# First batch's x loaded in whole rows into one tile for two steps, and step 1's first-stage groups moved out of the border into the head and units 0 to 2 of step 0

## The chip, the core and the metric

One Trainium2 chip, of which the program uses one core. The metric is the device time in microseconds of one execution; a kernel's time is the median of several runs. One execution is also recorded by the hardware profiler, and all rows below are from that one. All times inside the kernel count from the first instruction of its span.

## What is computed

Three stages in float32 follow one another: a convolution by FFT along the sequence (8 batches of 3072 positions, 256 channels), a soft mixture of experts on the 24576 rows that come out, and a gated feed-forward block. Cut to what matters:

```python
def _attn_ref(x, filt_r, filt_i):                 # x: (8, 3072, 256), filters: (1537, 256)
    X = np.fft.rfft(x, axis=1)
    Y = X * (filt_r + 1j * filt_i)[None, :, :]
    return np.fft.irfft(Y, n=x.shape[1], axis=1)

def _moe_ref(x, phi, w1, w2):                     # x: (24576, 256), phi: (256, 32)
    logits = x @ phi
    d = softmax(logits, axis=0)                   # over the rows; slot_input = d.T @ x
    slot_out = relu(slot_input @ w1[e]) @ w2[e]   # 8 experts with 4 slots each
    return softmax(logits, axis=1) @ slot_out

def _moe2_ref(x, w_gate, w_val, w_out):
    g = x @ w_gate
    return (g * sigmoid(g) * (x @ w_val)) @ w_out
```

## The kernel before

The program has two phases, with a short transition between them. Phase 1 (the first 380 us or so) does the Fourier part and the reduction to expert slots; phase 2 does the gated block, on PE from end to end. The change touches the first 65 us of phase 1.

**Steps and units.** Phase 1 runs over 16 *steps*; step s is batch s // 2 and half s % 2 of the 256 channels. Each step has a *first stage*: the sequence of 3072 positions is cut as 48 x 64, and a DFT over the 48 is done in four *chunks* of 32 channels each (s1_chunk). A chunk is four matmuls into a PSUM tile s (L235), a transpose by DVE into sg (L243), and a copy by ACT into the step's tile b (spread, L252). All four chunks of a step must be in b before its *second stage*, which runs in six *units* (s2_unit): four matmuls X<-fwd,b (L263), two products by DVE with the filter ft (P at L267, Q at L268), and two combinations by GpSimd into yt (L276, L280). Two units later the results are turned by PE (T, L290, tr_unit), and every second unit is multiplied with phi (L, L298, phi_pair); both are evacuated by ACT.

**Filters.** The filter tile ft is itself made on the chip: load_filters fetches six tiles fraw, and turn_filters transposes four blocks on PE (fT, L202), from where ACT (L209) and DVE (L214, L216) copy them into ft. The six groups of the first channel half are turned ahead of step 0, those of the second half one by one in the units of step 0.

**x.** load_x(step, k) issues on SP two of a step's four transfers (L182): for k = 0 or 1 and for r = 0 and 1, 48 partitions (0 to 47, or 64 to 111) with 16 pieces of 128 floats, since a step uses half of the channels of a row. Two pools xp[0] and xp[1], of 16 KB in each partition, hold the x of even and odd steps. Step 0 is loaded first of all, then come the filters and fwd, then step 1, and step s + 2 is issued in units 0 and 2 of step s.

**Order.** The order of the instructions on each engine is the order in which they are written (a manual schedule), each engine works its queue off in order, and what an engine waits for is set by the tiles. SP issues all of these transfers, and reuses eight semaphores in turn, so a transfer also waits for the landing of the one eight places before it. Ahead of the first chunk, ten *idle* matmuls of a constant keep PE busy while x is on its way. In units of a step s from 1 on, chunks of step s + 1 are spread over the units by the tables late and plan, one PSUM buffer for all of them, except for the odd chunks of the first three steps, which use the buffer of the tag c. Step 1's chunks have no place in a unit: they stand in a row in **border**, which comes behind the last unit of step 0, with the last filter group and two of the T groups and an L that are due there; step 1's first unit begins behind it.

**Later uses.** The pool cvp, behind the x pools, holds the raw weights of the gated block, which are converted from unit 14 on (conv); inv, the constants of the inverse transform, is fetched at unit 8.

Of the kernel before, what the change touches and what calls it, by code (L numbers as in the profile page):

```python
# [80 lines left out]
def spectral_softmoe_glu_kernel(  # L81
# [56 lines left out]
    def phase1():  # L138
        with ExitStack() as c1:
# [3 lines left out]
            xp = []  # L143
            cvs = ExitStack()
            yp = [c1.enter_context(tc.tile_pool(name=f"yp{k}", bufs=1)) for k in range(3)]
# [27 lines left out]
            def load_x(step, k):  # L173
                b, h = divmod(step, 2)
                if b >= NB:
                    return

                if k == 0:
                    xt[step] = xp[step % 2].tile([128, 2, 16, 128], F32, tag="x", name="x")
                xr = x[b].rearrange("(p h r n) d -> r h p n d", h=2, r=2, n=16)  # L180
                for r in range(2):
                    nc.sync.dma_start(  # L182
                        out=xt[step][64 * r:64 * r + 48, k], in_=xr[r, k, :, :, h * 128:(h + 1) * 128]
                    )

            def load_filters():
# [34 lines left out]
            def s1_chunk(step, c):  # L221
# [4 lines left out]

                if step < 3 and c % 2:
                    ps = ps_c.tile([128, 1024], F32, tag="c", name="s1").rearrange("p (n d) -> p n d", d=32)
                else:
                    ps = ps_s1.tile([128, 32, 32], F32, tag="s1", name="s1")  # L230
# [17 lines left out]
            def spread():  # L248

                while staged:  # L250
                    step, c, sg = staged.pop(0)
                    act.copy(  # L252
                        bt[step][:, :, c * 32:(c + 1) * 32].rearrange("p (j k) d -> p j k d", k=2),
                        sg[:, 0:NJ // 2].rearrange("p j d k -> p j k d"),
                    )
# [358 lines left out]
            def conv():  # L614
# [6 lines left out]
                def load(n):  # L621
                    if n >= len(chunks):
                        return
                    i, c = chunks[n]
                    raws[n] = cvp.tile([128, cw, 2], I32, tag="raw", name="raw", bufs=2)
                    nc.sync.dma_start(
                        out=raws[n].rearrange("p n k -> p (n k)"),
                        in_=flat((w_gate, w_val, w_out)[i])[:, c * cw:(c + 1) * cw].bitcast(I32),
                    )
# [4 lines left out]
                for n, (i, c) in enumerate(chunks):  # L634
# [3 lines left out]
                    pair = (lambda a: a.rearrange("p (h m) -> p h m", h=2)) if i == 2 else (lambda a: a)  # L638
                    mag = cvp.tile([128, cw], I32, tag="mag", name="mag", bufs=2)
                    low = cvp.tile([128, cw], I32, tag="low", name="low", bufs=2)  # L640
                    act.activation(pair(mag.bitcast(F32)), halves(hf), AF.Copy, scale=2.0 ** -112)
# [63 lines left out]
            act.copy(expo, expo)  # L705
            xp += [cr.enter_context(tc.tile_pool(name=f"xp{k}", bufs=1, side="right")) for k in (1, 0)][::-1]
            cvp = cvs.enter_context(tc.tile_pool(name="cvp", bufs=1, side="right"))
            load_x(0, 0)
            load_x(0, 1)
            load_filters()  # L710
# [3 lines left out]
            for k in range(2):  # L714
                nc.sync.dma_start(out=fwd[:, 12 * k:12 * k + 12], in_=c_fwd[:, 12 * k:12 * k + 12])
                if k == 0:
                    nc.sync.dma_start(out=phi_sb, in_=phi.rearrange("(t p) e -> p t e", p=128))
            load_x(1, 0)
            load_x(1, 1)
            idle = ps_x.tile([128, 512], F32, tag="X", name="idle")  # L720
            for _ in range(10):
                pe.matmul(out=idle[:, 0:384], lhsT=ident, rhs=csm)
            for c in range(4):
                s1_chunk(0, c)
                spread()
            for q in range(6):
                turn_filters(0, q)
# [4 lines left out]
            units = [(s, u) for s in range(2 * NB) for u in range(6)]  # L732
            late = [[[], [], [], [], [], []], [[], [], [0], [1], [2, 3], []]]
            plan = [[], [0], [1], [2], [3], []]
# [24 lines left out]

            def border():  # L760

                turn_filters(1, 5)
                s1_chunk(1, 0)
                s1_chunk(1, 1)
                spread()
                s1_chunk(1, 2)
                tr_unit(0, 3)
                s1_chunk(1, 3)
                spread()
                phi_pair(0, 1)  # L770
                tr_unit(0, 4)
                bt.pop(0)

            def aside():
                next(side, None)

            for i, (s, u) in enumerate(units):
                if u in (0, 2):
                    load_x(s + 2, u // 2)
# [4 lines left out]
                s2_unit(s, u)  # L784
                if i == 5:
                    border()
                    continue
                if s == 0:
                    turn_filters(1, u)
                spread()  # L790
                if i != 6:
                    tail_ops(i)
                if i >= CONV_AT and i % 2 == 0:
                    aside()
                pump(1)
                for c in (plan if s > 1 else late[s])[u]:
                    s1_chunk(s + 1, c)
                if u == 5:
                    bt.pop(s)
# [440 lines left out]
```

## Time and profile before

| | |
|---|---|
| median of 3 runs | 1443.76 us (1441.32 to 1445.64) |
| profiled execution, its own time | 1444.62 us |
| its span, first to last instruction | 1442.2 us |
| PE busy | 98% of the span |
| x of step 0 has landed | 15.50 us |
| first X matmul of step 0, step 1, step 2 | 25.07, 45.87, 60.65 us |

The page gives busy shares of the engines over the span and in 40 slices of 36 us each; the slice rows show at a glance where an engine is not busy, and how many GB/s the transfers moved. The chain of work that ended last tells, for a stretch, what each moment was waiting for. A view of stretches gives the busy time of each engine, the granted clock and the transfer rate between two points in time. A timeline lists instructions in order with the idle time before each and what ended it. PE is the matmul engine, PEld its weight loads, SPq the queue of SP that issues transfers.

### The profile page before, as it was taken

To read this page: it belongs to the slowest core of one execution; us is meant where nothing else is said; L and a number is where in the kernel's file an instruction comes from. 1 tells how busy PE (TensorE), PEld (TensorE's weight loads), DVE (VectorE), ACT (ScalarE), POOL (GpSimd) and SP (SyncE) were. 2 spreads that over 40 slices of the span, in tenths; PEclk is the share of its full clock that TensorE was granted. 3 is DMA by queue.
4 is the path that set the end of the run, shared out by engine and by line. 5 is a ranking of instruction groups with operands and counts; after the bars stand their busy time and mean duration, and the time that the engine had idled before them with its cause. 6 is when DMAs were issued, how large, how long until landed. Compare 5 with 4: busy or idle time off the path is not lost.

```text
span 1442.2 us, 22675 instructions
## 1 busy us (share of the span) xinstructions
PE 1410.8 (98%) x8441; PEld 1099.1 (76%) x8441; DVE 1139.3 (79%) x1760; ACT 911.1 (63%) x1673; POOL 258.7 (18%) x334
## 2 busy tenths in 40 slices
PE   7999999999999999999999999999999999999998
PEld 4566666656488888888888888888888888888887
DVE  4777888777388888878987897888789788877776
ACT  3567667764366667666666766676666667666664
POOL 1577677653210000000000000000000000000000
PEclk9999999999999999999999999999999999999999
DMA  9978988869811221221032023013111221221111
GB/s 227 184 138 156 158 146 136 169 152 375 281 28 30 44 55 30 44 55 30 16 73 41 15 37 78 15 30 65 35 30 30 59 41 29 45 45 26 19 30 30
DMA packets 178364, 116.25 MB, mean 81 GB/s; under 512 B 105264, under 2 KB 161456, under 8 KB 178128
## 3 DMA queue, kind: packets, MB, share of 16 engines
q1 hardware_dynamic: 176768, 112.92, 38.8%
q10 hardware_dynamic: 1104, 1.11, 0.3%
q8 instruction: 66, 1.08, 0.3%
q0 software_dynamic: 384, 0.79, 0.2%
q14 instruction: 42, 0.34, 0.1%
HBM read 68.13 MB, written 34.60 MB: 71 GB/s over the span
## 4 chain that ended last, share of the span: by engine, by line
PE 88%; DVE 5%; DMA 4%; ACT 2%; issue 1%; POOL 0%; SPq 0%; ACTq 0%; DVEq 0%; POOLq 0%
PE o L1115 53%; PE V L1078 9%; PE G L1077 9%; PE X L263 4%; PE s L235 3%; PE T L290 2%; DMA raw<-in_moe_w_out_dram 2%; DVE sg L243 1%; PE c L531 1%; PE L L298 1%; DMA x<-in_x_dram 1%; PE o L1135 1%; DMA fwd<-in_const_fwd_dram 1%; DVE P L267 1%; PE c L371 1%
## 5 line engine op out<-in xcount | busy, mean ns | idle before, releaser
L1115 PE MATMUL o<-hi,wo 128*128 128x512 f32 x2256 | 694.6, 389 | 0.0
L1080 ACT ACTIVATE s<-G 128x512 f32<-128x512 f32 x576 | 344.5, 598 | 328.2 <-PE G L1077 324.3
L1086 DVE TENSOR_TENSOR h<-V,s 128x512 f32<-128x512 f32 x576 | 393.7, 684 | 152.7 <-ACT s L1080 150.1
L1115 PEld LDWEIGHTS o<-hi,wo 128*128 128x128 f32 x2256 | 423.5, 188 | 87.6
L1115 PE MATMUL o<-lo,wo 128*128 128x512 f32 x1128 | 438.9, 389 | 0.3 <-DVE lo L1094 0.3
L1094 DVE TENSOR_TENSOR lo<-h,hi 128x512 fp32r<-128x512 f32 x576 | 419.8, 729 | 0.7
L1093 ACT CAST hi<-h 128x512 fp32r<-128x512 f32 x576 | 354.1, 615 | 36.8 <-DVE h L1086 35.2
L1115 PEld LDWEIGHTS o<-lo,wo 128*128 128x128 f32 x1128 | 211.8, 188 | 44.9 <-DVE lo L1094 0.7
L1078 PE MATMUL V<-c,v 128*128 128x512 f32 x576 | 224.6, 390 | 1.6 <-DVE h L1086 1.6
L1077 PE MATMUL G<-c,g 128*128 128x512 f32 x576 | 224.5, 390 | 0.3 <-ACT s L1080 0.3
L263 PEld LDWEIGHTS X<-fwd,b 128*128 128x128 f32 x768 | 92.9, 191 | 55.9 <-issue 38.4
L1078 PEld LDWEIGHTS V<-c,v 128*128 128x128 f32 x576 | 108.0, 188 | 25.5 <-DVE h L1086 3.5
L1077 PEld LDWEIGHTS G<-c,g 128*128 128x128 f32 x576 | 108.0, 188 | 24.2 <-ACT s L1080 1.2
L243 DVE STREAM_TRANSPOSE sg<-s 128x1024 f32<-128x1024 f32 x64 | 78.7, 1235 | 53.0 <-PE s L235 52.1
L1029 POOL TENSOR_TENSOR lg<-lg,mx 96x1024 f32<-96x1024 f32 x7 | 16.8, 2403 | 555.3 <-DVE mx L1027 555.3
L263 PE MATMUL X<-fwd,b 128*128 128x128 f32 x768 | 108.8, 285 | 3.6 <-ACT b L252 3.5
L252 ACT COPY b<-sg 128x768 f32<-128x768 f32 x64 | 59.1, 923 | 69.1 <-DVE sg L243 69.1
L276 POOL TENSOR_TENSOR yt<-P 128x256 f32<-128x256 f32 x96 | 70.4, 733 | 104.7 <-DVE P L267 103.6
L1120 DVE STREAM_TRANSPOSE ot<-o 128x512 f32<-128x512 f32 x94 | 65.0, 713 | 29.5 <-PE o L1115 29.5
L235 PE MATMUL s<-x,csm 48*64 48x512 f32 x512 | 72.6, 611 | 3.6 <-DVE sg L243 3.4
L267 DVE TENSOR_TENSOR P<-X,ft 128x512 f32<-128x512 f32 x96 | 64.7, 674 | 10.1 <-PE X L263 9.2
L280 POOL TENSOR_TENSOR yt<-Q 128x256 f32<-128x256 f32 x95 | 69.8, 734 | 0.4
(207 smaller groups left out, 991.5 us busy)
## 6 DMA issues: line engine op xcount, KB each, us to landing
x<-in_x_dram SPq DMA_DIRECT2D x64, 384.0 KB, 8.5
out_dram<-ot SPq DMA_DIRECT2D x188, 128.0 KB, 2.8
w<-in_moe_w_dram SPq DMA_DIRECT2D x16, 512.0 KB, 7.9
w<-in_moe_w_dram SPq DMA_DIRECT2D x8, 1024.0 KB, 11.1
c<-ch SPq DMA_DIRECT2D x42, 128.0 KB, 2.4
c<-cl SPq DMA_DIRECT2D x42, 128.0 KB, 2.4
raw<-in_moe_w_gate_dram SPq DMA_DIRECT2D x12, 256.0 KB, 5.5
raw<-in_moe_w_val_dram SPq DMA_DIRECT2D x12, 256.0 KB, 5.5
```

The source lines that it names most:

```text
L235: pe.matmul(out=ps[64 * k:64 * k + 64, 16 * r:16 * r + 16, :], lhsT=s1t_sb[64 * r:64 * r + 48, :], rhs=xt[step][64 * r:64 * r + 48, k, :, ...
L243: dve.transpose(out=sg.rearrange("p j d k -> p d j k"), in_=ps.rearrange("p n d -> p d n"))
L263: pe.matmul(out=ps[:, g].rearrange("p r m -> p (r m)"), lhsT=bb[:, j, :], rhs=fwd[:, j, :])
L267: dve.tensor_tensor(out=P, in0=ps, in1=f, op=ALU.mult)
L276: pool.tensor_tensor(out=y[:, :, 0, :], in0=P[:, :, 0, :], in1=P[:, :, 1, :], op=ALU.subtract)
L1077: pe.matmul(out=pg, lhsT=g4[c][:, fs], rhs=c4[b][:, q, G, :])
L1078: pe.matmul(out=pv, lhsT=v4[c][:, fs], rhs=c4[b][:, q, G, :])
L1080: act.activation(s, pg, AF.Silu)
L1086: dve.tensor_tensor(out=h, in0=pv, in1=s, op=ALU.mult)
L1093: act.copy(hi, h)
L1094: dve.tensor_tensor(out=lo, in0=h, in1=hi, op=ALU.subtract)
L1115: pe.matmul(out=a[h], lhsT=w[:, k, h], rhs=m, start=(f == 0 and n == 0), stop=(f == NF - 1 and n == 2), skip_group_check=True,)
```

## The change

The first batch's x is now fetched by load_pair into one tile x01 with room for both halves of the channels (32 KB in each partition, where later both x pools lie): four transfers, each of 48 partitions with one contiguous piece of 16 KB. Steps 0 and 1 read their halves of it. The x pools and cvp are opened (open_xp) behind unit 2 of step 0, when step 1's last chunk has been issued, and x of step 2 is issued there, all four transfers at once. The function border is gone: step 1's chunk 0 is done in the head, ahead of the filter transposes, chunks 1 to 3 in units 0 to 2 of step 0 through the table late, and the T and L groups go into the ordinary places (tail_ops). Six idle matmuls are issued instead of ten. The odd chunks of step 1 use the common PSUM buffer, since the other one serves the filter groups there.

```diff
             xp = []
-            cvs = ExitStack()
+            cvs, x01, cvps = ExitStack(), ExitStack(), []
...
+            def load_pair():
+
+                t = x01.enter_context(tc.tile_pool(name="x01", bufs=1, side="right")).tile(
+                    [128, 2, 16, D], F32, tag="x01", name="x01"
+                )
+                xr = x[0].rearrange("(p h r n) d -> r h p n d", h=2, r=2, n=16)
+                for k in range(2):
+                    for r in range(2):
+                        nc.sync.dma_start(out=t[64 * r:64 * r + 48, k], in_=xr[r, k])
+                for h in range(2):
+                    xt[h] = t[:, :, :, h * 128:(h + 1) * 128]
+
+            def open_xp():
+
+                x01.close()
+                xp.extend(
+                    [cr.enter_context(tc.tile_pool(name=f"xp{k}", bufs=1, side="right")) for k in (1, 0)][::-1]
+                )
+                cvps.append(cvs.enter_context(tc.tile_pool(name="cvp", bufs=1, side="right")))
...
-                if step < 3 and c % 2:
+                if step in (0, 2) and c % 2:
...
-            xp += [cr.enter_context(tc.tile_pool(name=f"xp{k}", bufs=1, side="right")) for k in (1, 0)][::-1]
-            cvp = cvs.enter_context(tc.tile_pool(name="cvp", bufs=1, side="right"))
-            load_x(0, 0)
-            load_x(0, 1)
+            load_pair()
             load_filters()
...
-            load_x(1, 0)
-            load_x(1, 1)
             idle = ps_x.tile([128, 512], F32, tag="X", name="idle")
-            for _ in range(10):
+            for _ in range(6):
                 pe.matmul(out=idle[:, 0:384], lhsT=ident, rhs=csm)
             for c in range(4):
                 s1_chunk(0, c)
                 spread()
+            s1_chunk(1, 0)
+            spread()
...
-            late = [[[], [], [], [], [], []], [[], [], [0], [1], [2, 3], []]]
+            late = [[[1], [2], [3], [], [], []], [[], [], [0], [1], [2, 3], []]]
...
-            def border():
-
-                turn_filters(1, 5)
-                s1_chunk(1, 0)
-                s1_chunk(1, 1)
-                spread()
-                s1_chunk(1, 2)
-                tr_unit(0, 3)
-                s1_chunk(1, 3)
-                spread()
-                phi_pair(0, 1)
-                tr_unit(0, 4)
-                bt.pop(0)
...
-                if u in (0, 2):
+                if s and u in (0, 2):
                     load_x(s + 2, u // 2)
                 if i == 8:
                     nc.sync.dma_start(out=inv, in_=c_inv)
                 if i >= CONV_AT and i % 2:
                     aside()
                 s2_unit(s, u)
-                if i == 5:
-                    border()
-                    continue
                 if s == 0:
                     turn_filters(1, u)
                 spread()
-                if i != 6:
-                    tail_ops(i)
+                tail_ops(i)
                 if i >= CONV_AT and i % 2 == 0:
                     aside()
                 pump(1)
                 for c in (plan if s > 1 else late[s])[u]:
                     s1_chunk(s + 1, c)
+                if i == 2:
+                    open_xp()
+                    load_x(2, 0)
+                    load_x(2, 1)
```

On SP, from the start of phase 1 (x and x_145 are loads of x, fraw and nyq filters, fwd, phi_sb and inv constants). Before:

```order
L182 DMA x<-in_x_dram 48x16x128 x4
L192 DMA fraw<-in_filt_r_dram 128x1024
...
L192 DMA fraw<-in_filt_i_dram 128x1024
L711 DMA nyq<-in_filt_r_dram 128x2x1
L715 DMA fwd<-in_const_fwd_dram 128x1536
L717 DMA phi_sb<-in_moe_phi_dram 128x2x32
L715 DMA fwd<-in_const_fwd_dram 128x1536
L182 DMA x<-in_x_dram 48x16x128 x12
L781 DMA inv<-in_const_inv_dram 128x3072
```

After, at the same place:

```order
L194 DMA x_145<-in_x_dram 48x4096 x4
L212 DMA fraw<-in_filt_r_dram 128x1024
...
L212 DMA fraw<-in_filt_i_dram 128x1024
L728 DMA nyq<-in_filt_r_dram 128x2x1
L732 DMA fwd<-in_const_fwd_dram 128x1536
L734 DMA phi_sb<-in_moe_phi_dram 128x2x32
L732 DMA fwd<-in_const_fwd_dram 128x1536
L182 DMA x<-in_x_dram 48x16x128 x8
L784 DMA inv<-in_const_inv_dram 128x3072
```

The four first transfers are twice as large, and the transfers of x behind fwd are eight instead of twelve; the first of these eight waits for PE.

On PE in the head and the first two units of step 0 (s is a chunk's PSUM tile, fT a filter group, X a unit's). Before:

```order
L722 MATMUL idle<-csm 128x384 x10
L235 MATMUL s_189<-x,csm 64x512 x4
L235 MATMUL s_197<-x,csm 64x512 x4
L235 MATMUL s_205<-x,csm 64x512 x4
L235 MATMUL s_213<-x,csm 64x512 x4
L202 MATMUL fT<-csm,fraw 128x128 x24
L263 MATMUL X<-fwd,b 128x128 x4
L202 MATMUL fT<-csm,fraw 128x128 x4
L263 MATMUL X<-fwd,b 128x128 x4
```

After:

```order
L737 MATMUL idle<-csm 128x384 x6
L255 MATMUL s_174<-x_145,csm 64x512 x4
L255 MATMUL s_182<-x_145,csm 64x512 x4
L255 MATMUL s_190<-x_145,csm 64x512 x4
L255 MATMUL s_198<-x_145,csm 64x512 x4
L255 MATMUL s_207<-x_145,csm 64x512 x4
L222 MATMUL fT<-csm,fraw 128x128 x24
L283 MATMUL X<-fwd,b 128x128 x4
L222 MATMUL fT<-csm,fraw 128x128 x4
L255 MATMUL s_298<-x_145,csm 64x512 x4
L283 MATMUL X<-fwd,b 128x128 x4
```

A fifth chunk stands ahead of the filter groups, and the next one behind unit 0.

On PE from the last unit of step 0 to the first units of step 1. Before, the border's chunks stand in a row:

```order
L263 MATMUL X<-fwd,b 128x128 x4
L202 MATMUL fT<-csm,fraw 128x128 x4
L235 MATMUL s_440<-x,csm 64x512 x4
L235 MATMUL s_447<-x,csm 64x512 x4
L235 MATMUL s_456<-x,csm 64x512 x4
L290 MATMUL T<-csm,yt 128x128 x4
L235 MATMUL s_470<-x,csm 64x512 x4
L298 MATMUL L<-yt,phi_sb 32x256 x4
L290 MATMUL T<-csm,yt 128x128 x4
L263 MATMUL X<-fwd,b 128x128 x8
```

After:

```order
L283 MATMUL X<-fwd,b 128x128 x4
L222 MATMUL fT<-csm,fraw 128x128 x4
L310 MATMUL T<-csm,yt 128x128 x4
L318 MATMUL L<-yt,phi_sb 32x256 x4
L283 MATMUL X<-fwd,b 128x128 x4
L310 MATMUL T<-csm,yt 128x128 x4
L283 MATMUL X<-fwd,b 128x128 x4
```

The chunks are gone from here, and one T has moved behind the first unit of step 1.

## Rows read from the trace of the kernel before

**Rows 1.** The page: span, PE's busy time, busy tenths in 40 slices.
```profile
span 1442.2 us, 22675 instructions
...
PE 1410.8 (98%) x8441; PEld 1099.1 (76%) x8441; DVE 1139.3 (79%) x1760; ACT 911.1 (63%) x1673; POOL 258.7 (18%) x334
...
PE   7999999999999999999999999999999999999998
```

**Rows 2.** Chain that ended last, first 65 us: start, us, what.
```profile
2.30 13.18 DMA x<-in_x_dram
15.50 9.53 DMA fwd<-in_const_fwd_dram
25.07 1.17 PE X L263 x8
...
37.34 1.06 PE s L235 x6
...
44.94 0.89 ACT b L252
45.87 2.05 PE X L263 x16
48.36 0.57 PE L L298 x8
48.93 1.09 PE X L263 x8
50.45 1.02 PE s L235 x8
...
60.65 1.16 PE X L263 x8
...
64.21 1.02 PE s L235 x8
```

**Rows 3.** Stretches, busy time by engine (instructions), granted clock, transfer share, GB/s.
```profile
4.00:14.00 10.00, 8.03 (x19) 4.66 (x20) 0.00 (x0) 0.00 (x0) 0.00 (x0) 1.00 1.25 149
15.00:22.00 7.00, 6.47 (x49) 2.73 (x43) 4.76 (x4) 3.16 (x4) 0.00 (x0) 1.00 1.04 405
27.00:37.00 10.00, 8.62 (x76) 7.56 (x76) 8.43 (x23) 4.00 (x13) 7.24 (x12) 1.00 1.25 154
380.00:382.00 2.00, 1.29 (x16) 0.61 (x8) 0.14 (x1) 1.29 (x2) 0.00 (x0) 1.00 1.11 355
383.00:386.00 3.00, 3.00 (x12) 1.05 (x11) 0.69 (x1) 0.58 (x1) 0.00 (x0) 1.00 1.05 216
```

**Rows 4.** Transfers issued, 370 to 390 us: count, KB each, us to landing.
```profile
wo<-wod SPq DMA_DIRECT2D x3, 512.0 KB, 9.6
c<-cd SPq DMA_DIRECT2D x4, 256.0 KB, 9.9
```

**Rows 5.** Timeline of PE, 14 to 50 us: start, us, instructions, idle before.
```profile
23.02 0.55 PE L202 MATMUL fT<-csm,fraw 128*128 128x128 f32 x3 [0.86 <-DMA fraw<-in_filt_i_dram]
24.35 0.63 PE L202 MATMUL fT<-csm,fraw 128*128 128x128 f32 x4 [0.78 <-DVE ft L216]
...
28.52 0.63 PE L202 MATMUL fT<-csm,fraw 128*128 128x128 f32 x4 [0.96 <-DVE ft L216]
...
30.29 0.63 PE L202 MATMUL fT<-csm,fraw 128*128 128x128 f32 x4 [0.25 <-DVE ft L216]
30.75 0.60 PE L290 MATMUL T<-csm,yt 128*128 128x128 f32 x4
...
45.87 2.05 PE L263 MATMUL X<-fwd,b 128*128 128x128 f32 x16 [1.20 <-ACT b L252]
```

**Rows 6.** Timeline of DVE, 14 to 50 us.
```profile
19.17 2.38 DVE L243 STREAM_TRANSPOSE sg<-s 128x1024 f32<-128x1024 f32 x2 [0.16 <-PE s L235]
...
30.14 0.69 DVE L267 TENSOR_TENSOR P<-X,ft 128x512 f32<-128x512 f32 x1
30.75 0.68 DVE L268 TENSOR_TENSOR Q<-X,ft 128x512 f32<-128x512 f32 x1
31.41 0.49 DVE L216 COPY ft<-fT 128x128 f32<-128x128 f32 x2
```

**Rows 7.** Timeline of SP's issuing, first 62 us.
```profile
0.74 4.64 SPq L182 DMA_DIRECT2D x<-in_x_dram  x4
...
15.50 0.33 SPq L715 DMA_DIRECT2D fwd<-in_const_fwd_dram  x1
...
19.12 30.41 SPq L182 DMA_DIRECT2D x<-in_x_dram  x12
```

**Rows 8.** Timeline of PE's weight loads, 5 to 18 us.
```profile
8.69 0.34 PEld L722 LDWEIGHTS idle<-csm 128*128 128x128 f32 x1 [0.30 <-issue]
9.33 0.34 PEld L722 LDWEIGHTS idle<-csm 128*128 128x128 f32 x1 [0.30 <-issue]
9.93 4.06 PEld L722 LDWEIGHTS idle<-csm 128*128 128x128 f32 x13 [0.26 <-issue]
```

More of the change, by code (lines that the diff above doesn't have):

```diff
@@ L624, in load @@
                     i, c = chunks[n]
-                    raws[n] = cvp.tile([128, cw, 2], I32, tag="raw", name="raw", bufs=2)
+                    raws[n] = cvps[0].tile([128, cw, 2], I32, tag="raw", name="raw", bufs=2)
                     nc.sync.dma_start(
@@ L638, in conv @@
                     pair = (lambda a: a.rearrange("p (h m) -> p h m", h=2)) if i == 2 else (lambda a: a)
-                    mag = cvp.tile([128, cw], I32, tag="mag", name="mag", bufs=2)
-                    low = cvp.tile([128, cw], I32, tag="low", name="low", bufs=2)
+                    mag = cvps[0].tile([128, cw], I32, tag="mag", name="mag", bufs=2)
+                    low = cvps[0].tile([128, cw], I32, tag="low", name="low", bufs=2)
                     act.activation(pair(mag.bitcast(F32)), halves(hf), AF.Copy, scale=2.0 ** -112)
```

## The prediction

> **What bounds the kernel now.** I read the page first, then the chain of work that ended last in the first 65 us, then the stages one by one. PE is busy 98% of a 1442.2 us span, and every slice after the first shows nine tenths or more; only the first slice (36 us) has a seven [rows 1]. A change in the head can thus gain only where PE waits, and once PE's queue is full again, a delay or a gain at that point is carried unchanged to the end. The reader is to see in the chain [rows 2] what the head waits for: the x transfer up to 15.50, then fwd up to 25.07, where step 0's second stage begins; from there on it is mostly PE, with the border (37.34 to 45.87) as the one place where PE, DVE and ACT hand over in turn. I measure everything at one marker: the first X matmul of step 2, at 60.65, behind which both kernels issue the same instructions.
>
> **Load of the first batch.** Before, four transfers bring step 0's half (4 x 384 KB = 1.573 MB), four more later bring step 1's. Now four transfers of 768 KB (3.146 MB) come first, and all of x must land before the first s matmul. What rate do they get? The view of stretches [rows 3] has the half-row loads of x, 512-byte pieces to 48 partitions, at 149 and 154 GB/s; filters and fwd, 4 and 6 KB pieces to 128 partitions, at 405. Piece length or number of partitions? Two stretches of the transition separate them: wo, in 1 KB pieces to 128 partitions, still runs at 355, while c<-cd, 4 KB pieces to only 32 partitions, gets 216 (which transfers these are, with their sizes: [rows 4]). So long pieces don't bring 400 GB/s where few partitions are written. The changed load writes long pieces to 48 partitions at a time, which no row shows. Bounds: 154 (same partitions, short pieces) and 405 (long pieces, all partitions); with the 216 of the long pieces to 32 partitions in between. The nearest are 154 and 216, and I take 175: the load keeps its partitions, and these seem to set the rate.
> [...]
>
> **When x lands.** The first packet moves at about 2.30 [rows 2]. Before, x landed at 15.50: 13.20 us, of which 1.573 MB / 154 GB/s = 10.2 are the bytes and 3.0 the constants' transfer beside it and the tail. Now 3.146 / 175 = 18.0, plus 3.0: x lands at 23.3, or 7.8 later. Bounds: 20.4 + 3.0 (25.7) and 7.8 + 1 to 3 (11.1 to 13.1).
>
> **From x to the first X matmul.** Before, 25.07 - 15.50 = 9.57: four chunks, paced by DVE's transposes (two in 2.38 us, [rows 6]), 24 filter transposes, and the wait for fwd; both end together, since the copies of ft hold the last filter transposes until 24.35 [rows 5]. fwd's first transfer is issued only when x's last has landed (15.50, [rows 7]), so in the new kernel it lands some 9.57 after x as well and is hidden by the longer chain. The fifth chunk in the head (step 1's first) adds one DVE transpose, 1.25. ACT's copy of it follows ahead of the filter copies and shifts with it. First X matmul: 23.3 + 9.57 + 1.25 = 34.1.
> **PE's clock.** [...] Six idle matmuls instead of ten end long before 23.3. [...] First X matmul at 35.1, +10.0.
>
> **Step 0 and the border.** Removed is the border: four chunks, two T groups and an L between 37.34 and 45.87, where PE waits for DVE and, last, 1.20 for ACT's copy of b [rows 5]. Before, first X matmul of step 0 to that of step 1: 45.87 - 25.07 = 20.80. Now the six units (37.34 - 25.07 = 12.27 before) take in three chunks of 1.05 (3.15), one T (0.50) and one L (0.57): 16.49 if PE fills no wait. In units 1 and 2 PE waited 0.96 + 0.25 for the copies of ft [rows 5], which a chunk can now fill; on the other side DVE has P 0.61, Q 0.61, ft 0.49 and a transpose of 1.25 in such a unit, 3.0 in all [rows 6], against PE's X 1.09, fT 0.5 and chunk 1.05, 2.6, so DVE sets the pace there for two units. Between 15.3 and 16.5 I take 16.0: -4.8. The second T goes into step 1's first unit: +0.5. Step 1's chunks all use one PSUM buffer now; with one chunk per unit (over 2 us apart) that costs nothing.
>
> **x of step 2.** Before, it was issued early and moved right behind step 1's half [rows 7], so chunk 0 of step 2 found it at 50.45. Now its buffer is part of the pair's tile: SP issues it when the last s matmul of step 1 has read that tile, at the end of unit 2. Counted from the first X matmul that is 8.4 (3 x 1.09 X, 3 x 0.5 fT, 0.5 T, 3 x 1.05 s). From issue to the last landing such a load took 15.50 - 0.74 = 14.8 on an idle queue [rows 2, 7]: ready at 23.2. The chunk is due at 16.0 + 4.58 (45.87 to 50.45) + 0.5 = 21.1. PE waits 2.1, with everything behind the s matmul in its queue. Behind the load on SP stand x of step 3, ready 10.2 later at 33.4 and due 3.6 behind the marker (64.21 - 60.65), at 16.0 + 15.3 (60.65 - 45.87, and the 0.5) + 2.1 + 3.6 = 37.0, then inv and raw: no wait. Bounds of the stall: 0 (PE reaches the chunk later) to 4. The pair's tile is what costs this: from fwd's landing to that issue nothing is in the queue, some 9 us.
>
> **Sum at the marker.** +10.0 - 4.8 + 0.5 + 2.1 = +7.8. The profiled execution took 1444.62 (span 1442.2), which gives 1452.4; it lies 0.86 above the median of 1443.76, so the median to expect is 1451.6, say 1452. Ends: the load at 216 GB/s (-3.4) with no clock loss (-1.0), no stall (-2.1) and 15.3 for step 0 (-0.7) gives +0.6; at 154 (+2.4), 2.1 of clock (+1.1), a stall of 4 (+1.9) and 16.5 (+0.5) it gives +13.7. Not all ends come at once: its own range is 1446 to 1457.
>
> **Rivals.**
> A: long pieces set the rate. At 405 GB/s x lands at 11.1 to 13.1, in the middle at 12.1, soon after six idle matmuls would end, and the first X matmul is at 22.9 (-2.2): -2.2 - 4.8 + 0.5 + 2.1 = -4.4, down to -6.5 without the stall: 1437 to 1441, in the middle 1439.4, **faster**. For it: every transfer with pieces of 4 KB and more to 128 partitions runs at 400 [rows 3]. Against: c<-cd's 216. It decides from some 290 GB/s on, where the sum is zero (10.7 + 3.0, x at 16.0, half of the clock's loss).
> B: the two partition halves overlap. Transfers to partitions 0 to 47 and 64 to 111 alternate in the queue; if the transfer engines spread over both, say 250 GB/s: 12.6 + 3.0, x at 17.9, the clock loses 0.5, first X matmul at 29.2 (+4.1): +4.1 - 4.8 + 0.5 + 2.1 = +1.9, 1445.7, **no change**. Against: the half-row loads alternate just so and get 154.
> C: x of step 2 comes later still, 5 us late instead of 2.1, or x of step 3 and the raw weights behind it also hold PE: 1455 to 1460.
>
> **How the numbers follow.** A measurement tells about 0.3% (4.3 us) from no change. Forecast 0.65 (0.59 of it slower, 0.06 within), A 0.16 (0.12 faster, 0.04 within), B 0.14 within, C 0.05 slower: faster 0.12, within 0.24, slower 0.64. The forecast's own 1446 to 1457 holds some 0.62; taking in B's lower half and a part of C, 1443 to 1458 holds 0.8, and what is left out is nearly all A.
>
> **What would show it.** In the new profile: GB/s near 155 to 215 from 3 to about 20 us, not 400; first s matmul on x at 21 to 26; first X matmul of step 0 at 31 to 37; then no border, step 1's first X matmul 15 to 16.5 later; a PE wait on x of 0 to 4 us at step 2's first chunk; marker at 66 to 71 instead of 60.65. An x that lands before 14 makes the forecast wrong; a border gain of less than 3 would make it too small.

## The result and the profile of the changed kernel

The changed kernel takes 1458.18 us (median of 4 runs, 1456.08 to 1459.89), the kernel before 1443.95 on the same chip: ratio 1.0099, 95% interval 1.0077 to 1.0122. It is slower, as forecast, but by 14 us where the forecast said 8: its 1452 was 6 too low, and the median lies just above the upper end of 1458. The profiled execution took 1459.47 us, with a span of 1457.7 against 1442.2.

The page of the changed kernel answers to [rows 1]: span, PE's busy time, its busy tenths in 40 slices, and the granted clock in tenths.

```profile
span 1457.7 us, 22650 instructions
...
PE 1416.7 (97%) x8433; PEld 1101.1 (76%) x8433; DVE 1139.0 (78%) x1760; ACT 911.5 (63%) x1673; POOL 258.8 (18%) x334
...
PE   5999999999899999999999999999999999999998
...
PEclk8999999999999999999999999999999999999999
```

The first slice has fallen from seven tenths to five, and there the granted clock reads eight tenths. PE is also busy for 5.9 us longer with eight matmuls fewer: some of them ran at a granted clock of 0.50 (27 to 38 us, below). The chain that ended last (start, us, what) answers to [rows 2]:

```profile
2.10 24.45 DMA x<-in_x_dram
26.59 8.79 PE s L255 x34
35.38 4.10 PE fT L222 x20
...
50.20 12.46 DMA x<-in_x_dram
62.71 1.07 PE s L255 x2
...
72.95 1.16 PE X L283 x8
```

Before, the chain waited for x until 15.50 and then for fwd until 25.07. Now x takes until 26.56, fwd is not in the chain, and PE itself is: 34 s matmuls and 20 filter transposes in a row, 12.9 us. The stretches (busy time by engine, then granted clock, transfer share, GB/s) answer to [rows 3]:

```profile
4.00:14.00 10.00, 3.98 (x6) 2.18 (x7) 0.00 (x0) 0.00 (x0) 0.00 (x0) 1.00 1.03 148
15.00:22.00 7.00, 3.49 (x11) 0.95 (x9) 0.00 (x0) 0.00 (x0) 0.00 (x0) 0.99 0.96 138
...
27.00:34.00 7.00, 7.00 (x30) 1.55 (x26) 3.97 (x4) 2.41 (x3) 0.00 (x0) 0.50 1.04 404
34.00:38.00 4.00, 4.00 (x21) 2.69 (x14) 2.29 (x2) 2.35 (x6) 0.10 (x1) 0.50 0.74 289
40.00:55.00 15.00, 14.39 (x122) 10.59 (x120) 13.65 (x31) 7.11 (x21) 7.47 (x13) 1.00 0.41 54
```

The whole rows move at 148 and 138 GB/s, no faster than the half rows did (149 and 154), and twice the bytes have to come. In the two stretches behind (27 to 38) PE is busy all the time at a granted clock of 0.50. PE's timeline (start, us, instructions, idle time before them) shows what it did ahead of that; it answers to [rows 5, 8]:

```profile
10.02 6.61 PE L737 MATMUL idle<-csm 128*128 128x384 f32 x12 [10.02 <-DMA csm<-in_const_small_dram]
16.57 1.07 PE L255 MATMUL s<-x,csm 48*64 48x512 f32 x2
21.15 1.30 PE L255 MATMUL s<-x,csm 48*64 48x512 f32 x4 [3.51 <-DMA x<-in_x_dram]
26.59 4.43 PE L255 MATMUL s<-x,csm 48*64 48x512 f32 x13 [4.15 <-DMA x<-in_x_dram]
...
39.99 1.06 PE L283 MATMUL X<-fwd,b 128*128 128x128 f32 x8
...
55.73 1.16 PE L283 MATMUL X<-fwd,b 128*128 128x128 f32 x8
...
62.71 1.07 PE L255 MATMUL s<-x,csm 48*64 48x512 f32 x2 [0.88 <-DMA x<-in_x_dram]
...
72.95 1.16 PE L283 MATMUL X<-fwd,b 128*128 128x128 f32 x8 [0.56 <-ACT b L272]
```

The idle matmuls are over at 16.6; then PE stands for 3.51 and 4.15 us between a few s matmuls. The border is gone: from step 0's first X matmul (39.99) to step 1's (55.73) no long wait is left. x of step 2 does hold PE, and by more than the 0.88 us of idle time in its row: the last two matmuls of that chunk take as long alone (1.07) as all eight together elsewhere (1.09). SP's issuing (start, us, what) answers to [rows 7]:

```profile
26.56 0.33 SPq L732 DMA_DIRECT2D fwd<-in_const_fwd_dram  x1
...
48.67 15.16 SPq L182 DMA_DIRECT2D x<-in_x_dram  x8
```

| stage, us | before | forecast | changed kernel | miss |
|---|---|---|---|---|
| all of x has landed | 15.50 | 23.3 | 26.56 | +3.3 |
| from there to the first X matmul | 9.57 | 11.8 | 13.43 | +1.6 |
| step 0's first X to step 1's | 20.80 | 16.0 | 15.74 | -0.3 |
| step 1's first X to step 2's | 14.78 | 17.4 | 17.22 | -0.2 |
| step 2's first X, later than before | 0 | +7.8 | +12.30 | +4.5 |

Two of the four terms were right within 0.3 us and two were too small; their misses make up the 4.5 us. Behind the marker the shift grows from 12.30 to 15.65 at step 15 (352.55 against 336.90 for the X matmuls of its last unit), where the forecast had nothing.

### The profile page after: what moved, and what is told of

The parts are those of the page before. It is cut to its first block, busy times and chain, and to the rows that moved or that the text cites. A ratio compares the mean times of both kernels' runs of the same rounds, so it can differ in the third digit from the quotient of the medians.

```text
span 1457.7 us, 22650 instructions
## 1 busy us (share of the span) xinstructions
PE 1416.7 (97%) x8433; PEld 1101.1 (76%) x8433; DVE 1139.0 (78%) x1760; ACT 911.5 (63%) x1673; POOL 258.8 (18%) x334
## 4 chain that ended last, share of the span: by engine, by line
PE 86%; DVE 5%; DMA 5%; ACT 2%; issue 2%; POOL 1%; SPq 0%; ACTq 0%; DVEq 0%
PE o L1118 52%; PE V L1081 9%; PE G L1080 9%; PE X L283 3%; PE s L255 3%; DMA x<-in_x_dram 3%; PE T L310 2%; DVE sg L263 1%; PE c L551 1%; DMA raw<-in_moe_w_gate_dram 1%; DMA raw<-in_moe_w_out_dram 1%; PE L L318 1%; DVE P L287 1%; PE o L1138 1%; PE c L391 1%
## 5 line engine op out<-in xcount | busy, mean ns | idle before, releaser
L255 PE MATMUL s<-x,csm 48*64 48x512 f32 x512 | 78.0, 647 | 11.1 <-DMA x<-in_x_dram 8.5
L311 ACT COPY y<-T 128x512 f32<-128x512 f32 x96 | 56.4, 588 | 21.8 <-PE T L310 21.8
```

Of the source, the lines that this page charges most:

```text
L255: pe.matmul(out=ps[64 * k:64 * k + 64, 16 * r:16 * r + 16, :], lhsT=s1t_sb[64 * r:64 * r + 48, :], rhs=xt[step][64 * r:64 * r + 48, k, :, ...
```

## The experiments

Each kernel ran beside the kernel before on the same chip (medians of that: 1444.55 to 1445.46; 1443.95 for the first row). The table gives the stages of the table above from each profiled execution (x has landed when the matmul that waited for its last part starts, or SP issues behind it, which agree within 0.12; in e4 and e5 PE is still busy then and does not show it, so SP's issue is taken), step 2's first X against before (marker), and the median and the ratio with its interval.

| run | x landed | x to first X | step 0 | step 1 | marker | median | ratio |
|---|---|---|---|---|---|---|---|
| changed kernel | 26.56 | 13.43 | 15.74 | 17.22 | +12.30 | 1458.18 | 1.0099 (1.0077 to 1.0122) |
| e6, again | 25.31 | 13.42 | 15.74 | 19.06 | +12.88 | 1456.42 | 1.0083 (1.0065 to 1.0102) |
| e1, 128 partitions | 13.88 | 10.71 | 15.74 | 17.28 | -3.04 | 1441.93 | 0.9981 (0.9970 to 0.9993) |
| e7, 64 partitions | 23.54 | 13.43 | 15.73 | 17.10 | +9.15 | 1454.60 | 1.0077 (1.0053 to 1.0100) |
| e2, half rows | 25.27 | 9.57 | 16.62 | 16.27 | +7.08 | 1454.89 | 1.0076 (1.0059 to 1.0092) |
| e3, two queues | 24.81 | 13.43 | 15.74 | 16.74 | +10.07 | 1457.10 | 1.0086 (1.0071 to 1.0101) |
| e4, 22 idle matmuls | 25.54 | 10.71 | 15.74 | 18.90 | +10.24 | 1454.59 | 1.0070 (1.0055 to 1.0085) |
| e5, order alone | 14.64 | 10.71 | 15.74 | 15.27 | -4.29 | 1440.56 | 0.9974 (0.9964 to 0.9983) |
| e8, filled, by SP | 88.98 | 12.40 | 15.73 | 17.26 | +73.72 | 1518.61 | 1.0510 (1.0490 to 1.0531) |
| e11, filled, by GpSimd | 28.72 | 11.91 | 15.74 | 17.23 | +12.95 | 1456.48 | 1.0079 (1.0051 to 1.0107) |
| e12, e11 and earlier | 28.81 | 15.60 | 15.16 | 15.28 | +14.20 | 1457.65 | 1.0083 (1.0065 to 1.0101) |

(e9 is told with e8.)

**Is it the partitions or the pieces that set the load's rate?** Two runs change the number of partitions that a transfer writes and keep long pieces.

```diff
-                xr = x[0].rearrange("(p h r n) d -> r h p n d", h=2, r=2, n=16)
-                for k in range(2):
-                    for r in range(2):
-                        nc.sync.dma_start(out=t[64 * r:64 * r + 48, k], in_=xr[r, k])
+                xr = x.rearrange("b s d -> (b s) d")[0:4096].rearrange("(p a) d -> p a d", p=128)
+                tf = t.rearrange("p k n d -> p (k n) d")
+                for j in range(4):
+                    nc.sync.dma_start(out=tf[:, 8 * j:8 * j + 8], in_=xr[:, 8 * j:8 * j + 8])
```

> The changed kernel, but the four first transfers write 8 KB pieces to all 128 partitions (4.19 MB in all, a third more than the pair), so x holds other numbers than the first batch's; all instructions of the engines stay. Theory (the 48 partitions set the rate of the pair's load): some 400 GB/s in the stretch from 3 to 12 us, first chunk at 13 to 14.5 instead of 26.6, granted clock without a drop, first X matmul of step 0 at 24 to 25.5 instead of 39.99, first X matmul of step 2 at 57 to 59 instead of 72.95, time 1441 to 1445. Rival (long pieces, or 3 to 4 MB ahead of the filters, are slow whatever the partitions): first chunk still behind 22, time above 1452.

```diff
-                xr = x[0].rearrange("(p h r n) d -> r h p n d", h=2, r=2, n=16)
+                xr = x.rearrange("b s d -> (b s) d")[0:4096].rearrange("(k r p n) d -> r k p n d", k=2, r=2, n=16)
...
-                        nc.sync.dma_start(out=t[64 * r:64 * r + 48, k], in_=xr[r, k])
+                        nc.sync.dma_start(out=t[64 * r:64 * r + 64, k], in_=xr[r, k])
```

> The pair's load by four transfers of 1 MB to 64 partitions each (0 to 63 and 64 to 127, in turn; 16 KB pieces as now), 4.19 MB in place of 3.146 MB; x comes from other rows, so the results are those of another input. [...] Rival (a transfer to one half of the partitions has about 137 GB/s whatever the number of partitions): x at 33 to 35, step 2's first X at 79 or later, time 1463 or more.

The stretch from 4 to 14 us, of e1 and then of e7 (its last two numbers are the transfer share and GB/s):

```profile
4.00:14.00 10.00, 7.58 (x18) 3.64 (x22) 0.00 (x0) 0.00 (x0) 0.00 (x0) 1.00 1.01 422
```

```profile
4.00:14.00 10.00, 6.64 (x14) 2.99 (x13) 0.00 (x0) 0.00 (x0) 0.00 (x0) 1.00 1.02 211
```

The same tile takes 422 GB/s over 128 partitions (8 KB pieces), 211 over 64 and 138 to 148 over 48 (16 KB pieces; e6, the changed kernel again, has 153 and 150 in the two stretches). The transfer share is 1.0 in all three (1.01, 1.02, and 0.96 to 1.03), so the engines that carry the transfers are occupied and yet move less; no run here says why. e7 moves a third more bytes than the changed kernel and has them 3.0 us sooner than its first profile and 1.8 sooner than e6. e1's theory held with its numbers, and e7's rival is refuted: 211 GB/s and x at 23.54, not 137 and 33 to 35. With a fast load the rest of the change is worth -3.0 us at the marker.

**Do half rows, a second queue or the clock change it?**

```diff
-                for k in range(2):
-                    for r in range(2):
-                        nc.sync.dma_start(out=t[64 * r:64 * r + 48, k], in_=xr[r, k])
+                for h in range(2):
+                    for k in range(2):
+                        for r in range(2):
+                            nc.sync.dma_start(
+                                out=t[64 * r:64 * r + 48, k, :, h * 128:(h + 1) * 128],
+                                in_=xr[r, k, :, :, h * 128:(h + 1) * 128],
+                            )
```

> The changed kernel, with the pair's tile filled by eight half-row transfers (512-byte pieces, first the half of step 0) in place of four whole-row ones; bytes and partitions as in the changed kernel. Theory (48 partitions set the rate, pieces of 16 KB bring nothing or even cost): all of x there at 24 to 27, as 26.6 now, time within 4 us of the changed kernel's 1458. Rival (long pieces are faster, and something else delayed x): x there after 28, time above 1461. If step 0's chunks may start when their own half has landed, the first is at about 15.5 and the fifth waits for the other half.

The stretches of e2's half rows, and then of the whole rows in e6:

```profile
4.00:14.00 10.00, 7.87 (x18) 3.63 (x18) 0.00 (x0) 0.00 (x0) 0.00 (x0) 1.00 1.25 152
15.00:22.00 7.00, 6.36 (x28) 1.50 (x28) 4.16 (x4) 2.67 (x3) 0.00 (x0) 0.64 1.25 156
```

```profile
4.00:14.00 10.00, 4.35 (x9) 2.55 (x10) 0.00 (x0) 0.00 (x0) 0.00 (x0) 1.00 1.00 153
15.00:22.00 7.00, 3.13 (x7) 0.48 (x6) 0.00 (x0) 0.00 (x0) 0.00 (x0) 0.81 0.98 150
```

All of x is there at 25.27, as in e6 (25.31), so whole rows are no faster than half rows: pieces of 16 KB bring nothing where 48 partitions are written, as the theory had it. Since step 0's half comes first, its four chunks run while the rest loads, and the first X matmul stands 9.57 behind x, where it waits for fwd, and not 13.42 behind it. The granted clock is at 0.50 there too (22 to 26 us, and the first eight X matmuls still take 2.08 us where the next take 1.16); the wait for fwd hides what that costs. Of these 3.9 us step 0 gives back 0.9 (16.62).

```diff
-                        nc.sync.dma_start(out=t[64 * r:64 * r + 48, k], in_=xr[r, k])
+                        (nc.scalar if r else nc.sync).dma_start(out=t[64 * r:64 * r + 48, k], in_=xr[r, k])
```

> The changed kernel, with the two transfers to partitions 64 to 111 issued by ACT and the two to partitions 0 to 47 by SP, so that both halves of the partitions are in flight together. Theory (both halves take turns on one queue, and each gets its own limited rate): the rate from 3 to 15 us rises from about 140 to over 200 GB/s, x there at 14 to 20, time 1446 to 1453. Rival (the transfer engines work them off in turn whatever the queue): x there at 24 to 27, time 1455 to 1461.

x lands 0.5 us before that of e6 and 1.75 before that of the changed kernel, at 173 GB/s from 4 to 14 us and 154 from 15 to 22 (with one queue 148 and 138, and 153 and 150 in e6): the second queue brings little, and this run's rival held. The 250 GB/s of rival B were not reached.

```diff
-            for _ in range(6):
+            for _ in range(22):
                 pe.matmul(out=idle[:, 0:384], lhsT=ident, rhs=csm)
```

> The changed kernel with 22 idle matmuls instead of 6, so that PE is busy until x lands. Theory (the granted clock of 0.50 from 22 to 39 us costs 2.6 us between x and the first X matmul): x still there at 26 to 27, granted clock 1.00 throughout, first X matmul 10.8 behind x instead of 13.4, time 2 to 3 us below the changed kernel's: 1455 to 1456.5. Rival (the slow stretch is hidden by DVE's transposes and the filters): first X matmul 13 behind x, time as the changed kernel's, 1457 to 1459.

The timeline of PE, SP's issue behind x and some stretches of this run (granted clock third from the end) show what they do, and a second place where the clock falls:

```profile
9.56 15.87 PE L737 MATMUL idle<-csm 128*128 128x384 f32 x44 [9.56 <-DMA csm<-in_const_small_dram]
25.36 2.12 PE L255 MATMUL s<-x,csm 48*64 48x512 f32 x16
...
59.05 1.07 PE L255 MATMUL s<-x,csm 48*64 48x512 f32 x2 [0.96 <-DMA x<-in_x_dram]
```

```profile
25.54 0.34 SPq L732 DMA_DIRECT2D fwd<-in_const_fwd_dram  x1
```

```profile
22.00:26.00 4.00, 4.00 (x18) 2.24 (x20) 0.00 (x0) 0.00 (x0) 0.00 (x0) 1.00 0.75 188
...
60.00:62.00 2.00, 2.00 (x11) 1.96 (x11) 1.25 (x1) 0.50 (x1) 0.00 (x0) 0.56 1.26 156
62.00:64.00 2.00, 2.00 (x16) 0.84 (x18) 1.29 (x2) 1.09 (x3) 1.15 (x2) 0.59 1.24 157
64.00:66.00 2.00, 2.00 (x19) 1.24 (x12) 1.10 (x1) 0.26 (x1) 0.99 (x2) 1.00 1.26 145
```

With the idle matmuls reaching almost to x's landing, the granted clock stays at 1.00 in the head and 16 s matmuls take 2.12 us, where the changed kernel needs 4.43 for 13. From x to the first X matmul it is now 10.71; the four profiles with PE idle before a load of whole rows and a clock of 0.50 to 0.56 from 26 to 36 us have 13.4 (the changed kernel, e3, e6, e7). So the head's clock costs 2.7 us. It costs less where the clock comes back sooner: e8 and e11 (below) leave PE idle before x too, but have 0.80 from 90 to 100 us and 1.00 from 33 to 39 us, and take 12.4 and 11.9. Behind the wait for x of step 2 (0.96 us of idle time before 59.05) the clock of e4 falls again (0.56 and 0.59 from 60 to 64 us), which the theory did not have, and 1.7 of the gain are lost there. e6 shows the same (below); the changed kernel's own profile does not. x (25.54) and the time (1454.59) lie 0.4 to 0.5 below what was expected.

**What is the new order worth without the load?**

```diff
-                    xt[step] = xp[step % 2].tile([128, 2, 16, 128], F32, tag="x", name="x")
+                    xt[step] = xp[(step + (step > 1)) % 2].tile([128, 2, 16, 128], F32, tag="x", name="x")
...
-            load_pair()
+            open_xp()
+            load_x(0, 0)
+            load_x(0, 1)
+            xt[1] = xt[0]
...
-            for _ in range(6):
+            for _ in range(10):
...
-                if s and u in (0, 2):
+                if u in (0, 2):
                     load_x(s + 2, u // 2)
...
-                if i == 2:
-                    open_xp()
-                    load_x(2, 0)
-                    load_x(2, 1)
...
-                    wt = xp[k].tile([128, 2, 2, FE], F32, tag="x", name="w")
+                    wt = xp[1 - k].tile([128, 2, 2, FE], F32, tag="x", name="w")
```

> The new order of the chunks alone, with the load of before: only step 0's half of x is loaded, in half rows as before, with ten idle matmuls as before; step 1's chunks read step 0's half again (step 1's own half is left out, so its results are those of another input), and the x pools are open from the start, so that x of step 2 is issued in units 0 and 2 of step 0. Theory: the border's removal is worth what its stages measured, whenever x lands. x at 15.5, first X matmul of step 0 at 26.3 (25.07 of before, and 1.25 for the fifth chunk's transpose), step 1's first X 15.7 later at 42.0, no wait for x of step 2, step 2's first X 15.3 later at 57.3 (before 60.65): -3.3, time 1440 to 1442. Rival: in the changed kernel the shorter step 0 only took back what the late x had cost, DVE becomes the bound once x is early: step 0 takes 17 or more, step 2's first X at 60 or later, time 1443 to 1446.

PE's timeline of this run, and SP's issue behind x:

```profile
14.29 2.31 PE L255 MATMUL s<-x,csm 48*64 48x512 f32 x16
...
25.35 1.06 PE L283 MATMUL X<-fwd,b 128*128 128x128 f32 x8
...
41.09 1.16 PE L283 MATMUL X<-fwd,b 128*128 128x128 f32 x8
...
56.36 1.16 PE L283 MATMUL X<-fwd,b 128*128 128x128 f32 x8 [0.56 <-ACT b L272]
```

```profile
14.64 0.34 SPq L735 DMA_DIRECT2D fwd<-in_const_fwd_dram  x1
```

Step 0 takes 15.74 to the hundredth as in the changed kernel, though x came 12 us earlier: the border's removal is worth 5.06 us in step 0 whenever x lands, and the rival falls; the time is in the theory's 1440 to 1442. Of the 5.06, step 1 takes back 0.49 (15.27 against 14.78 before) and the fifth chunk in the head 1.14 (10.71 against 9.57), so 3.4 us are left. Without a late x of step 2, step 1 takes 15.27, so the wait for it costs 1.95 in the changed kernel. The run's x was there at 14.64, 0.86 earlier than before, which was not expected and not followed up; without that the marker would be at -3.4, near the expected -3.3.

**Is the later growth of the shift part of the change?**

The changed kernel, unaltered, a second time.

> The changed kernel a second time, for a second profile. Theory (the 3.3 us that came behind step 2's first X are of that one execution): x lands again at 25.4 to 26.6, step 2's first X again 11 to 12.5 us later than before, but what comes behind that differs by -1.5 to +1.6 as in the other runs, and the median stays at 1456 to 1460. Rival (the late raw weights hold ACT in every execution of this kernel): the shift again grows by 2.5 to 3.5 us between step 2 and step 15, at steps 3, 6, 7 and 12.

The shift is +12.88 at the marker and +13.67 at step 15, so 0.8 us come behind it, not 3.3. Its x (25.31) and its marker lie just outside the expected 25.4 to 26.6 and 11 to 12.5. In both profiles of this kernel ACT waits here and there for raw weights (11.4 us in all from 60 to 360 us in the first; 0.96 before 113.94 and 0.75 before 147.47 in the second), and so it did before (9.6 us). In the first, the granted clock also fell at 180 to 190 us (0.73, 0.93); in the second it reads 1.00 there. The other runs have -1.5 to +1.6 there, but e8 (below) has +3.5. So the 3.3 are not of every execution of this kernel, and such a growth is not of this kernel alone. Where e6 differs is step 1, 19.06: behind the wait for x that ends at 61.72 (1.15 us of idle time) its clock is at half for a while.

```profile
62.00:64.00 2.00, 2.00 (x12) 1.28 (x11) 1.18 (x2) 0.00 (x0) 0.00 (x0) 0.94 1.26 135
64.00:66.00 2.00, 2.00 (x16) 0.84 (x18) 1.27 (x3) 1.57 (x3) 1.25 (x2) 0.50 1.27 127
66.00:68.00 2.00, 2.00 (x13) 0.60 (x6) 0.45 (x1) 0.18 (x1) 0.89 (x2) 0.71 1.23 137
```

**Can the right x come over all partitions?** Partitions 48 to 63 and 112 to 127 of the tile are read by nobody. Filled with other rows, each transfer spans 128 partitions.

```diff
-                xr = x[0].rearrange("(p h r n) d -> r h p n d", h=2, r=2, n=16)
                 for k in range(2):
-                    for r in range(2):
-                        nc.sync.dma_start(out=t[64 * r:64 * r + 48, k], in_=xr[r, k])
+                    for m in range(2):
+                        nc.sync.dma_start(
+                            out=t[:, k, 8 * m:8 * m + 8].rearrange("p n d -> p (n d)"),
+                            in_=bass.AP(x.tensor, (32 * k + 8 * m) * D, [[16 * D, 2], [64 * D, 64], [1, 8 * D]]),
+                        )
```

> The pair's load to all 128 partitions with the right data: each of the four transfers brings 48 partitions of either half and fills the 16 between with rows that nobody reads (4.19 MB in place of 3.146 MB, 8 KB pieces). Theory (the partitions set the rate, and that is what makes the change slow): over 400 GB/s as in the run with other data, all of x at 13 to 14.5, granted clock 1.00, step 2's first X at 57 to 58 (before 60.65), time 1440 to 1443, so no slower than before. Rival (a transfer whose source is in two strided parts goes no faster than those to 64 partitions, 213 GB/s): x at 22 or later, step 2's first X at 68 or later, 1452 or more.

The next has the same load, and the chunks earlier:

```diff
-            s1_chunk(1, 0)
-            spread()
+            for c in range(2):
+                s1_chunk(1, c)
+                spread()
...
-            late = [[[1], [2], [3], [], [], []], [[], [], [0], [1], [2, 3], []]]
+            late = [[[2], [3], [], [], [], []], [[], [], [0], [1], [2, 3], []]]
...
-                if i == 2:
+                if i == 1:
                     open_xp()
```

> As the run before in this call, and chunk 1 of step 1 in the head too, chunks 2 and 3 in units 0 and 1 of step 0, so that the pair's tile is free and x of step 2 issued one unit (3 us) earlier. Theory (what is left of the change's cost is the wait for x of step 2, 2.0 us with a fast load, as the tile is free late): that wait goes, the head grows by 0 to 1.25 us, a unit of step 0 without a chunk saves 0.5 to 1: step 2's first X at 54.5 to 57, time 1438 to 1441. Rival (the head is paced by DVE's transposes, the sixth chunk costs its 1.25 us and more, and DVE's work in step 0 stays): step 2's first X at 57 or later, no gain over the run before.

Both theories fell on the load: 1518.61 and 1520.75 us (e9: ratio 1.0522, 1.0503 to 1.0541), x at 88.98 and 89.28. Two rows of e8, of the load and of PE's wait for it:

```profile
20.00:30.00 10.00, 0.00 (x0) 0.00 (x0) 0.00 (x0) 0.00 (x0) 0.00 (x0) 0.50 0.13 52
```

```profile
88.98 6.13 PE L257 MATMUL s<-x,csm 48*64 48x512 f32 x30 [43.56 <-DMA x<-in_x_dram]
```

52 GB/s at a transfer share of 0.13, and 0.13 of sixteen engines is as much as two of them busy; the rate is the same from 20 to 50 us, and all four transfers (4.19 MB) take until 88.98. Their source pattern begins with a count of two (the two halves). That of e1, with the same pieces to the same partitions, begins with 128 and that of e7 with 64, and both have a share of 1.0 (422 and 211 GB/s). The rival's number (213 GB/s) is refuted as well; that the rate isn't the fast one it had right. Of the earlier chunks e9 tells the same as e12 below: step 1 takes 15.27 instead of 17.26, but the stretch from x to the first X takes 16.04 instead of 12.40, and step 2's first X is 1.4 us later than in e8. There its rival was right.

**The same load issued by GpSimd**, in eight transfers, with filters and fwd behind it on that queue; then with the chunks moved as in e9.

```diff
                 for k in range(2):
-                    for r in range(2):
-                        nc.sync.dma_start(out=t[64 * r:64 * r + 48, k], in_=xr[r, k])
+                    for m in range(4):
+                        nc.gpsimd.dma_start(
+                            out=t[:, k, 4 * m:4 * m + 4].rearrange("p n d -> p (n d)"),
+                            in_=bass.AP(x.tensor, (32 * k + 4 * m) * D, [[16 * D, 2], [64 * D, 64], [1, 4 * D]]),
+                        )
...
-                        nc.sync.dma_start(out=raw, in_=src[:, 4 * k:4 * k + 4, :])
+                        nc.gpsimd.dma_start(out=raw, in_=src[:, 4 * k:4 * k + 4, :])
...
-                nc.sync.dma_start(out=fwd[:, 12 * k:12 * k + 12], in_=c_fwd[:, 12 * k:12 * k + 12])
+                nc.gpsimd.dma_start(out=fwd[:, 12 * k:12 * k + 12], in_=c_fwd[:, 12 * k:12 * k + 12])
```

> The filled pair's load again (48 partitions of either half, 16 filler partitions, right data, 4.19 MB), but as eight transfers of 512 KB issued by GpSimd, with the filters and fwd behind them on the same queue. The run from SP moved 52 GB/s at a transfer share of 0.13, two of sixteen engines, since its source pattern begins with a count of two. [...] Rival (two parts in the source are slow whoever issues them): 52 to 60 GB/s again, x at 75 or later, time 1500 or more.

> As the run before in this call, with chunk 1 of step 1 in the head and chunks 2 and 3 in units 0 and 1 of step 0, so that the pair's tile is free and x of step 2 is issued one unit earlier (not to be read in the run from SP, where x took 89 us). Theory: the wait for x of step 2, 1.95 us in the changed kernel, goes, and the sixth chunk in the head costs 0 to 1.25 us: step 2's first X 0.5 to 2 us earlier than in the run before. Rival (the sixth chunk costs 1.25 or more, and step 0's units are paced by DVE): step 2's first X no earlier than in the run before.

The load in e11:

```profile
9.00:15.00 6.00, 1.16 (x4) 0.38 (x2) 0.00 (x0) 0.00 (x0) 0.00 (x0) 0.77 1.00 240
15.00:21.00 6.00, 0.00 (x0) 0.00 (x0) 0.00 (x0) 0.00 (x0) 0.00 (x0) 0.50 1.05 244
```

From GpSimd, with the same first count, the transfer share is 1.0 again and the rate 240 to 244 GB/s from 9 to 21 us; the rival of 52 GB/s falls. But it is just above half of e1's 422, it rises slowly (99 GB/s from 3 to 9 us, while GpSimd works on the eight issues until 7.7), and all of x lands at 28.72: later than in the changed kernel (26.56), and no gain. Why occupied engines move no more than that stays open.
In e12 the wait for x of step 2 is gone as expected (step 1 takes 15.28, as in e5), but the head grows by 3.7 us: by the sixth chunk, which waits 1.60 us for DVE before 38.32, and by a lower clock (0.50 from 28 to 32 us, then 0.56, 0.86 and, from 40 to 44, 0.71, where e11 has 1.00 from 33 to 39). It ends 1.25 behind e11; there its rival was right.

No version with the right x beat the kernel before. e1 and e5, which are faster than it, have x from other rows or leave half of it out.

## Why the prediction was right in sign and too small

**The load (step "What rate do they get?"): wrong by 3.3 us.** The reading that partitions and not pieces set the rate was right (422 GB/s to 128 and 211 to 64; to 48, 152 and 156 with the short pieces of e2), and rival A, long pieces at 405 GB/s, is refuted: 148 and 138, and 153 and 150 in e6. The size was not: 175 was taken between 154 (48 partitions, short pieces) and 216 (32 partitions, long pieces), as if longer pieces could only help. They gave nothing, and both profiles lie below 154, the bound that was called lower. By that bound x would have been put at 25.7; e6 has 25.31, e4 25.54, the first profile 26.56.

**From x to the first X: wrong by 1.6.** The chain itself was right: 9.57 + 1.25 = 10.82 against 10.71 in each of the runs with full clock (e1, e4, e5). The clock's 1.0 in the sum, and the 2.1 at its upper end, were the author's estimate, and no run shows them; the stretches from 27 to 38 show 0.50 over all five chunks and into the filter transposes, and that cost 2.7 in all (13.43 against 10.71). e4 shows that by taking it away. fwd was hidden, as said.

**Step 0 and the border: right.** 16.0 forecast, 15.74 measured in the changed kernel and, to 0.01, in eight of the nine other profiles that kept this order (e2 has 16.62); e5 shows that it doesn't hang on the late x.

**x of step 2: right.** 2.1 forecast, 1.95 by e5 against the changed kernel. The place too: the s matmul at 62.71, which x releases. The clock's fall behind it (0.56 and 0.59 in e4, 0.50 and 0.71 in e6, some 1.6 us beside the wait) was in no case.

**Behind the marker: 0 forecast.** 0.8 and 3.4 in the two profiles, with ACT late for raw weights as in rival C and, in one, a stretch of low clock; the other runs show both signs (-1.5 to +3.5), so this is scatter for the most part. With the marker it makes +15.65 and +13.67, near the +15.5 and +13.6 of the two spans; the medians are +14.2 and +11.9. The time lies in the range of rival C, 1455 to 1460, but by luck: x of step 2 did not come 5 us late, and most of the difference was made by the load and the clock.

**The range.** The load at 154 and the clock's loss at 2.1 were taken for ends that don't come together. Both hang on one cause: with x early the clock stayed at 1.00 (e1, e5), with x late PE stood idle before it and the clock fell to 0.50 (the changed kernel, e3, e6, e7), and with x late but PE kept busy it read 1.00 (e4). They did come together, which by the prediction's own terms is +11.3 (7.8 + 2.4 + 1.1); the first profile's x was another 0.9 later than that and its clock's loss 0.6 larger. That the median lies 0.18 above 1458 is within the scatter, since the same kernel had 1456.42 in e6; that 1452 was too low is not.

## What to carry to other kernels

A load's rate is read from rows with the same number of partitions and the same first count in its pattern; longer pieces stood in for neither here (138 to 153 GB/s with 16 KB pieces to 48 partitions, 52 with a first count of two). Where x came later, PE restarted at a granted clock of 0.50 behind the wait (the changed kernel, e3, e6, e7), so the clock's loss belongs to the same case as the lateness, not to an independent one. Taking a serial stretch out and filling its work into units with slack was worth 5 us in that stretch here, 3.4 with what the head and the next step took back, and could be priced to 0.3 us from the trace; the load that this needed, both halves of x at once, cost three times the 5 us (11.1 for its landing, 2.7 of clock, 2.0 for x of step 2 behind it).

## What the runs showed of the hardware

- Transfers of 8 KB pieces moved at 422 GB/s to 128 partitions (e1); those of 16 KB pieces at 211 to 64 (e7) and at 138 to 153 to 48 (the changed kernel, e6); half rows to 48 in 512-byte pieces at 149 to 156 (before, e2).
- A source pattern that begins with a count of two ran at 52 GB/s with a transfer share of 0.13 from SP (e8, e9), and, as eight transfers in flight together, at 240 to 244 with a share of 1.0 from GpSimd (e11).
- The small constants (192 KB, on ACT's queue) landed at 9.4 to 10.0 beside the 16 KB pieces to 48 partitions (the changed kernel, e3, e4, e6), at 5.7 and 5.9 in e1 and e2, and at 3.7 in e7; the idle matmuls that wait for them start as much later. No run tells why.
- Behind PE's wait for x of step 2 the granted clock read 0.50 to 0.71 over two stretches of 2 us in two profiles (e4, e6: step 1 takes 18.9 and 19.1). In six others with that wait step 1 takes 16.7 to 17.3: the changed kernel's reads 1.00 from 60 to 66 us, and in all six (it, e1, e3, e7, e8, e11) the eight X and the next eight s matmuls behind the wait take 1.16 and 1.09 us, where e4's X take 1.93 and e6's s 1.80.
